# A listed order for the first two groups, own places for chunks 2 to 5, and no unused products at the end

## The chip, the cores and the metric

The kernel runs on one core of a Trainium2 chip. Its time is device microseconds, the median of several runs. The engines are TensorE (PE in the profile, with PEld for its weight loads), VectorE (DVE), ScalarE (ACT), GpSimd (POOL) and SyncE (SP), which here only issues DMAs. Each works off its own queue in order and waits on semaphores for the others.

## The reference

Linear attention with decay, in blocks of 64 positions, feeds a two-layer product with a leaky ReLU. Inputs are q, k, v of (4, 8, 768, 64) in float32, lam per head, and w_in (512, 2048) and w_out (2048, 512) in float64.

```python
for b in range(nb):                       # blocks of 64 positions
    intra = (qb @ kb.T * Dmask) @ vb
    inter = (qb * lam_pow) @ kv_state
    out[b] = intra + inter
    kv_state = lam_block * kv_state + (kb * rev_pow).T @ vb
x = out as (3072 tokens, 512)
h = x @ w_in
g = maximum(0.01 * h, h)
return g @ w_out
```

## The kernel before

**Tiling.** Tokens are cut into 24 chunks of 128 (two blocks each), six to a batch entry; four chunks make a group of 512 tokens, so there are six groups. w_in is cut into eight pairs p of two blocks of 128 columns. The two large products are done in three terms (h, l and m parts of each operand, each rounded to what one pass of PE keeps), so one pair of one group costs 24 matmuls of 128x512: `up(g, p)`, six steps of four matmuls in line L640, two for each of h, l and m. Its result, after the leaky ReLU on ACT (L658, L661), goes through the buffers gs0 and gs1 to DRAM tiles G. After all groups the second product, `down`, reads them back (L700) and writes the output.

**A chunk** goes through these steps. Three loads (k and q as two DMAs of 128 KB each, L338; v as one of 256 KB, L388). `transposes`: k and q are transposed on PE (L403) and copied by ACT (L414, L415); k is scaled in place (L419) and q (L423). `scores`: the scores go to the lower halves of the two banks of psc and the k-v products to the upper halves (both L313); DVE then makes sc (L452) and adds the products to the running state (L457, L459), which POOL scales (L462). `outputs`: own part, first state part, a small read of po (L491), second state part (L313), then xh, xl, xm (L507, L508, L510), which are the moving operand of `up`.

**A half of w_in** (512 KB, one DMA, L566) lands in one of three places raw0 to raw2, is read by ACT three times (L578, L580, L582) and put together by DVE (L584, L585); with two halves there, L591 or L593 makes wh, L596 wl, L602 wm of that pair.

**Places.** k, q, v and their transposed forms of chunk c lie in place c % 2, so a load for chunk c waits until chunk c - 2 has done with them. All loads and stores go through SP's queue, in order.

**Order.** Nothing is issued as it is written. The class `Plan` collects every step with its engine, a cost and the names it reads and writes (`add`); `emit` then picks steps one by one, each time the one that could start first by these costs, and issues them in the order of the planned start times. Names are what it knows of dependencies: psc is one name. Where PE would wait over 0.4 us by the plan, `busy` puts in unused transposes (L266, called fillers here); 11 more run at the very start. Once a pair's product has been put in bank b10, no more are added. The weights come in the order p = 1, 0, 2, 3, 4, 7, 6, 5, and the first `up` is that of group 0 and p = 1, after chunks 0 to 3.

**The end.** After the last step 24 row-strip matmuls (L802) and eight small ones (16 with both halves in the trace, L809) write PSUM areas that nobody reads.

## Time and profile before

| | |
|---|---|
| median of three runs | 611.96 us (610.98 to 612.29) |
| span of the profiled execution | 610.3 us |
| lying around it (median less span) | 1.7 us; no other time of that execution is recorded |
| PE busy, share of the span | 601.9 us, 99% |
| DVE, ACT, POOL busy | 313.2, 269.9, 86.6 us |
| first product in L640 | at 30.41 us |
| unused transposes L266 | 30, the last at 26.8 us |

The page cuts the span into 40 slices; each digit is a busy share in tenths. A busy PE counts unused matmuls too, and matmuls of a stream overlap, so a mean of 389 ns for one of 128x512 stands for one each 227 ns. In the views, "x64" merges neighbours of one kind, and the bracket gives the idle time before an instruction and what ended it.

### The profile page before, as it was taken

To read this page: it belongs to the slowest core of one execution; us is meant where nothing else is said; L and a number is where in the kernel's file an instruction comes from. 1 tells how busy PE (TensorE), PEld (TensorE's weight loads), DVE (VectorE), ACT (ScalarE), POOL (GpSimd) and SP (SyncE) were. 2 spreads that over 40 slices of the span, in tenths; PEclk is the share of its full clock that TensorE was granted. 3 is DMA by queue.
4 is the path that set the end of the run, shared out by engine and by line. 5 is a ranking of instruction groups with operands and counts; after the bars stand their busy time and mean duration, and the time that the engine had idled before them with its cause. 6 is when DMAs were issued, how large, how long until landed. Compare 5 with 4: busy or idle time off the path is not lost.

```text
span 610.3 us, 13012 instructions
## 1 busy us (share of the span) xinstructions
PE 601.9 (99%) x5426; PEld 497.6 (82%) x5426; DVE 313.2 (51%) x418; ACT 269.9 (44%) x430; POOL 86.6 (14%) x90
## 2 busy tenths in 40 slices
PE   7799999999999999999999999999999999999999
PEld 5688888888888878888788888888888888888887
DVE  5899764334243426326366755545454544636531
ACT  4678974444455646555577522222222313214111
POOL 2564412114133004104000000000000000000000
PEclk9899999999999999999999999999999999999999
DMA  9999775666889878886686843524333343333201
GB/s 201 236 261 263 215 204 126 175 154 176 192 212 245 212 222 219 212 242 212 233 302 219 278 155 103 173 69 139 137 104 134 111 136 111 132 104 126 82 1 69
DMA packets 147754, 105.18 MB, mean 172 GB/s; under 512 B 123632, under 2 KB 124400, under 8 KB 147696
## 3 DMA queue, kind: packets, MB, share of 16 engines
q1 hardware_dynamic: 147552, 104.36, 58.8%
q8 instruction: 42, 0.69, 0.5%
q14 instruction: 16, 0.13, 0.1%
q10 hardware_dynamic: 144, 0.00, 0.0%
HBM read 68.69 MB, written 35.65 MB: 171 GB/s over the span
## 4 chain that ended last, share of the span: by engine, by line
PE 95%; DMA 2%; ACT 1%; DVE 1%; issue 0%; SPq 0%; ACTq 0%
PE b L640 42%; PE b L700 18%; PE po L700 11%; PE psc L700 11%; PE po L313 4%; PE psc L313 4%; PE pt L700 4%; DMA g<-gs 1%; DMA att<-in_v_dram 1%; PE pt L403 1%; DMA att<-in_q_dram 1%; PE po L403 0%; PE psc L802 0%; ACT att L415 0%; PE b L266 0%
## 5 line engine op out<-in xcount | busy, mean ns | idle before, releaser
L682 ACT ACTIVATE xh<-att 128x1024 fp32r<-128x1024 f32 x48 | 50.8, 1060 | 149.1 <-PE b L700 133.6
L683 DVE SCALAR_TENSOR_TENSOR xl<-att,xh 128x1024 fp32r<-128x1024 f32 x48 | 58.7, 1223 | 97.5 <-ACT xh L682 97.5
L640 PE MATMUL b<-xm,wm 128*128 128x512 f32 (+2 forms) x392 | 104.5, 392 | 0.7 <-ACT b L658 0.7
L640 PE MATMUL b<-xh,wh 128*128 128x512 f32 (+2 forms) x392 | 103.2, 386 | 0.8 <-ACT xh L507 0.8
L640 PE MATMUL b<-xl,wl 128*128 128x512 f32 (+2 forms) x392 | 103.4, 387 | 0.0
L640 PEld LDWEIGHTS b<-xh,wh 128*128 128x128 f32 x392 | 72.9, 188 | 16.0 <-ACT xh L507 0.9
L640 PEld LDWEIGHTS b<-xl,wl 128*128 128x128 f32 x392 | 72.7, 188 | 15.1 <-DVE wl L596 0.3
L640 PEld LDWEIGHTS b<-xm,wm 128*128 128x128 f32 x392 | 71.4, 188 | 16.0 <-ACT b L658 1.1
L658 ACT ACTIVATE b<-b 128x512 f32<-128x512 f32 (+2 forms) x97 | 56.1, 580 | 60.6 <-PE b L640 60.5
L661 ACT ACTIVATE gs<-b 128x512 f32<-128x512 f32 (+2 forms) x97 | 57.0, 592 | 44.2 <-PE b L640 38.3
L700 PE MATMUL b<-wh,xh 128*128 128x512 f32 x192 | 74.7, 389 | 0.0
L700 PE MATMUL b<-wl,xl 128*128 128x512 f32 x192 | 74.7, 389 | 0.0
L685 DVE SCALAR_TENSOR_TENSOR xm<-xl,xh 128x1024 fp32r<-128x1024 f32 x48 | 58.7, 1225 | 4.7
L462 POOL TENSOR_TENSOR att<-att 128x256 f32<-128x256 f32 x40 | 34.4, 861 | 58.7 <-DVE att L459 58.7
L700 PEld LDWEIGHTS b<-wh,xh 128*128 128x128 f32 x192 | 36.1, 188 | 7.5
L700 PEld LDWEIGHTS b<-wl,xl 128*128 128x128 f32 x192 | 36.0, 188 | 7.5
L423 POOL TENSOR_TENSOR att<-att 128x512 f32<-128x512 f32 (+1 forms) x20 | 25.3, 1265 | 95.6 <-PE po L313 34.7
L452 DVE TENSOR_TENSOR att<-psc,att 128x512 f32<-128x512 f32 x24 | 16.5, 689 | 43.1 <-PE psc L313 43.1
L584 DVE TENSOR_SCALAR w<-w 128x512 int32<-128x512 int32 x32 | 19.6, 612 | 36.0 <-ACT w L578 35.9
L700 PE MATMUL psc<-wh,xh 128*128 128x512 f32 x96 | 37.3, 389 | 0.0
L700 PE MATMUL psc<-wl,xl 128*128 128x512 f32 x96 | 37.3, 389 | 0.0
L700 PE MATMUL psc<-wm,xm 128*128 128x512 f32 x96 | 37.3, 389 | 0.0
(79 smaller groups left out, 810.4 us busy)
## 6 DMA issues: line engine op xcount, KB each, us to landing
att<-g SPq DMA_DIRECT2D x48, 512.0 KB, 3.3
g<-gs SPq DMA_DIRECT2D x47, 512.0 KB, 4.0
raw<-in_moe_w_in_dram SPq DMA_DIRECT2D x16, 512.0 KB, 5.5
raw<-in_moe_w_out_dram SPq DMA_DIRECT2D x16, 512.0 KB, 4.8
att<-in_k_dram SPq DMA_DIRECT2D x48, 128.0 KB, 4.3
att<-in_v_dram SPq DMA_DIRECT2D x24, 256.0 KB, 4.5
out_dram<-gs SPq DMA_DIRECT2D x23, 256.0 KB, 2.1
wo<-w SPq DMA_DIRECT2D x8, 512.0 KB, 5.9
```

The lines of the kernel that those rows point to most:

```text
L313: nc.tensor.matmul(dst[HALF[cols]], lhsT=lhsT[HALF[rows]], rhs=rhs[HALF[rows]], start=start, stop=True, skip_group_check=True)
L423: add(eng, us, lambda: e.tensor_tensor(o, x, _bc(pow_q, 2, 2)[:, :, m, :], op=ALU.mult), ["fq", dep], [f"qsT{i}"])
L452: add("DVE", 0.69, lambda: nc.vector.tensor_tensor(sc, psc[:, :, lower, :], decay, op=ALU.mult), ["psc", "fk"], ["sc"])
L462: add("POOL", 0.7, lambda new=new, j=j: nc.gpsimd.tensor_tensor(state[(j + 1) % 4], new, _bc(lam_c, 2, D), op=ALU.mult), [f"st{j % 4}", "f ...
L584: add("DVE", 0.42, lambda: nc.vector.tensor_scalar(d, d, 3, None, op0=ALU.logical_shift_left), [], [key])
L640: nc.tensor.matmul(dst, lhsT=w[z][:, kk * 2 * P + f * P:kk * 2 * P + (f + 1) * P], rhs=x[z][:, kk, toks], start=start and kk == 0, stop=kk ...
L658: add("ACT", ns, lambda b=b: nc.scalar.activation(out=b, in_=b, func=AF.Copy, bias=0.0, scale=S + 1.0), [], [kb], rank=-1.5)
L661: add("ACT", ns, lambda b=b, r=r: nc.scalar.activation(out=r, in_=b, func=AF.Prelu, bias=0.0, scale=1.0 / WS, alpha=0.01), [kb], [f"gs{jg} ...
L682: add("ACT", 1.05, lambda: nc.scalar.activation(out=h, in_=graw[j], func=AF.Copy, bias=0.0, scale=NEAR), reads, wr("h"))
L683: add("DVE", 1.25, lambda: nc.vector.scalar_tensor_tensor(l, graw[j], 1.0, h.bitcast(F32), op0=ALU.mult, op1=ALU.subtract), reads + [f"rh{ ...
L685: add("DVE", 1.25, lambda: nc.vector.scalar_tensor_tensor(m, l.bitcast(F32), -S, h.bitcast(F32), op0=ALU.mult, op1=ALU.add), [f"rh{j}", f" ...
L700: nc.tensor.matmul(acc[tb][z // 2][:, cols], lhsT=ring[j][z][:, f * T + tb * P:f * T + (tb + 1) * P], rhs=W[pp][z][:, f * d_model:(f + 1) ...
```

## The change

Four things change.

First, `ORDER` lists 711 steps: everything up to the last product of groups 0 and 1, with the loads, weights and attention steps that go with it. A number is a step's place in the order in which `add` was called, a letter says which engine takes it where there is a choice (a ACT, v DVE, p POOL), and f1 or f2 puts one or two fillers ahead of the next PE step. `emit` places these in the listed order, per engine, and goes on by its old rule after them; fillers by rule are off. The list has ten fillers besides the first eleven; the old order had 19.

To read its beginning: 2, 3, 4 are the loads of k, q, v of chunk 0; 25, 26, 27 those of chunk 1; 48, 49, 50 of chunk 2; 71, 72, 73 of chunk 3; 109, 110, 111 of chunk 4; 118, 119, 120 of chunk 5. 94 and 100 load the two halves of w_in's p = 1, 165 and 171 those of p = 0, 203 and 209 those of p = 2, 218 and 224 those of p = 3. 35, 58 and 80 are the k-v products and 34, 57 and 81 the scores of chunks 1, 2 and 3. 159 is the first product. 177 makes wh of p = 0 on DVE and 238 is the first product with it. 9p puts the scaling of chunk 0's k on POOL, where the old run had it on DVE.

The SP order of the loads up to the first product was k0 q0 v0 k1 q1 v1, half of p 1, q2 k2, half of p 1, v2 q3 k3 q4 v3, half of p 0, k4 q5 v4, half of p 0. In the list it is k0 q0 v0 k1 k2 q1 q2, half of p 1, v1 q3 v2, half of p 1, k3 v3, half of p 0, half of p 0, q4, half of p 2, k4.

Second, chunks 2 to 5 get places of their own, in the memory of the weights of p = 5, 6, 7 and 4, which are made last. A step without cost (write names of the chunk and of the weights) hands the memory over.

Third, the scores and the k-v products get names of their own, psS and psK, in place of psc, and the second part of the factors (`factors_q`) names the first as an input.

Fourth, the unused products at the end are gone.

```diff
+ORDER = """
+2 3 4 0 25 f1 5 48 1 9p f1 6 26 8 10 7 f1 12 49 f1 28 94 11 30 32p 27 13 72 14 15 f2 29 51 31 33 50 18 55 16 19
+34 20a 17 21 95 36 52 53 100 22 71 35 54 23 96 73 57 37 56 41 38 42 98 165 43a 39 44 59 58 40 45 97 75 60 46 61
+77 171 99 f1 64 102 110 47 65 101 79 66a 103 f1 67 104 74 68 105 203 76 78 62 106a 109 69 f1 81 63 80 82 83 87
+70 88 107 89a 90 91 108 167 f1 159 166 92 172 154 24 168 113 175 173 209 93 155 118 174 169 160 170 156 111 176
+157 218 161 447 177v 205 112 178 158 238 116 206 162 179 204 210 224 239 84 120 233 134 240 211 234 85 207 119
...
+"""
...
+        for i, e in self.listed:
+            e = e or next(iter(self.ops[i][0]))
+            assert i in able[e]
+            put(i, e, max(free[e], since(i, e)))
...
-                if self.idle is not None and t > soon[e] + 0.4:
+                if i in self.fill:
+                    self.idle(self.fill[i])
+                elif not self.listed and self.idle is not None and t > soon[e] + 0.4:
...
+    OWN = {2: 5, 3: 6, 4: 7, 5: 4}
...
-    W = [[sb([P, 4 * 2 * P], f"w{x}{p}", F32R) for x in "hlm"] for p in range(NP)]
+    def weights(p, dt=F32R):
+        return [sb([P, 4 * 2 * P], f"w{x}{p}", dt) for x in "hlm"]
+
+    W = [weights(p, F32 if p in OWN.values() else F32R) for p in range(NP)]
...
+    for p in OWN.values():
+        for j, (x, y) in enumerate(zip(kqv, (kTs, qTs, qsTs))):
+            z = W[p][j]
+            x.append(z[:, :H * D].rearrange("p (h d) -> p h d", h=H))
+            y.append(z[:, H * D:].rearrange("p (y t) -> p y t", y=HP))
...
-    add("DVE", 1.25, factors_q, [], ["fq"])
+    add("DVE", 1.25, factors_q, ["fk"], ["fq"])
...
-        return c // NCB, c % NCB, c % 2
+        return c // NCB, c % NCB, c % 2 if c not in OWN else 2 + list(OWN).index(c)
...
-            add("PE", 0.47, go, [f"kT{i}", f"qT{i}"], ["psc"])
-        add("PE", 0.47, kv, [f"k{i}", f"v{i}"], ["psc"])
+            add("PE", 0.47, go, [f"kT{i}", f"qT{i}"], ["psS"])
+        add("PE", 0.47, kv, [f"k{i}", f"v{i}"], ["psK"])
...
+        if p in OWN.values():
+            i = 2 + list(OWN.values()).index(p)
+            add("DVE", 0.0, lambda: W[p].__setitem__(slice(3), weights(p)), [],
+                [f"{x}{i}" for x in ("k", "q", "v", "kT", "qT", "qsT")] + [f"w{x}{p}" for x in "hlm"])
...
-    strips(2, 6)
-    strips(4, 3)
-    f = graw[0]
-    for _ in range(4):
-        for i in range(2):
-            nc.tensor.matmul(spare[2][HALF[i], 0:C2], lhsT=f[:, 0:C2], rhs=f[:, 0:C2], start=True, stop=True, skip_group_check=True)
```

More of the change, by code (lines that the diff above doesn't have):

```diff
@@ new lines @@
+157 218 161 447 177v 205 112 178 158 238 116 206 162 179 204 210 224 239 84 120 233 134 240 211 234 85 207 119
+86 212 208 241 115 114 213 127 235 214 128 163 215v 236 220 216 121 237 244 125 135 129 219 249 130 123 217 153
+131 242 245 221 222 225 164 250 117 180 246 132 136 223 251 247 323 226 149 181 252 227 228 122 133 138 229 124
+139 141 126 140a 143 230a 142 152 187 248 231 137 266 144 255 147 145 202 148 260 151 329 150 243 362 232 261
+267 182 262 184 325 195 185 188 186a 189 197 183 190 256 198 193 191 199 324 263 192 194 253 335 420 200 268
@@ new lines @@
+327 257 201 254 146 270 326 301 274 271 273 283 272a 275 328 300 258 276 330 277 350 289 259 278 288 331 290
+333 294 284 291 332 285 295 264 334 269 296 265 292 286 336v 356 287 297 293 337 280 339 196 279 344 338 340
+281 303 341 345 351 352 342 354 346 302 298 304 299 305 308 306v 468 483 309 307 469 310 347 343 311 353 366
+348 375 414 357 349 358 380 360 408 312 484 359 367 355 474 368 470 361 369 435 381 318 370 473 363a 319 376
+382 364 371 377 372 383 365 373 313 374 378 415 482 416 386 379 387 384 410 385 397 409 498 388 391 412 417 418
@@ new lines @@
+392 411 419 413 441 398 393 322 421v 389 480 399 422 477 394 390 475 317 479 402 395 320 314 423 472 403 436
+476 316 437 396 400 478 404 424 471 401 315 442 425 443 445 321 518 439 429 444 282 430 451 460 481 503 431 465
+499 426 458 500 438 456 502 501v 446 504 459 405 509 466 508 510 464 432 440 406 467 461 448v 427 457 449 407
+487 428 452 545 527 550 516 492 463 536 486 454 488 455 450 453 493 489 553 433 549 490 494 537 495 517 491 540
+555 496 462 505 543 560 506 434 561 671 566 589 546 562 515 547 556 485 551 511 497 563 557 526 590 552 538 581
@@ new lines @@
+558 521 591 548 512 592 559 541 513 542 594 593 524 514 564 528 595 567 568 570 588 569v 571 522 577 572 554
+620 573 578 532 596 582 539 579 621 574 529 576 534 625 580 622 533 626 520 544 601 525 604 531 602 519 605
+603v 507 606 530 597 585 523 535 623 598 565 627 599 689 607 631 608 690 619 586 616 628 600 611 691 610 692
+624 583 587 629 584 613 632 633 636 634v 637 650 694 638 648 675 614 693 672 651 695 653 649 659 639 700 661
+617 615 658 612 662 652 705 673 630 646 706 618 666 682 701 707 575 687 696 678 708 702 680 703 679 676 697 665
@@ L37 @@
+677 635 698 660 704 642 654 709 643 688 663 644 609 699 645 640 684 686 647 674 641 664 685 681 710 670 668 657
+655 667 669 656 683
+"""
 class Plan:
@@ L50, in __init__ @@
         self.cold, self.idle, self.spare = 6.0, None, None
+        self.listed, self.fill = [], {}
     def begin(self, name):
@@ L85, in emit @@
         follows, heads = {}, {}
+        first = {i for i, _ in self.listed}
         for c in self.chains.values():
+            if first.issuperset(c):
+                continue
             m = [i for i in c if "PE" in self.ops[i][0]]
@@ L113, in emit, with put @@
         done = []
-        while len(done) < n:
-            best = None
-            for e in free:
-                for i in able[e]:
-                    if e == "PE" and (i != locked[0] if locked else i in follows):
-                        continue
-                    t = max(free[e], since(i, e))
-                    if (best is None or (t, self.ops[i][3]) < best[:2]) and good(i, e, t):
-                        best = (t, self.ops[i][3], i, e)
-            t, _, i, e = best
+        def put(i, e, t):
             ways, fn = self.ops[i][:2]
-            if i in heads:
-                locked = list(heads[i])
-            elif locked and i == locked[0]:
-                locked.pop(0)
             for x in ways:
@@ L143, in emit @@
                         able[x].add(u)
+        for i, e in self.listed:
+            e = e or next(iter(self.ops[i][0]))
+            assert i in able[e]
+            put(i, e, max(free[e], since(i, e)))
+        while len(done) < n:
+            best = None
+            for e in free:
+                for i in able[e]:
+                    if e == "PE" and (i != locked[0] if locked else i in follows):
+                        continue
+                    t = max(free[e], since(i, e))
+                    if (best is None or (t, self.ops[i][3]) < best[:2]) and good(i, e, t):
+                        best = (t, self.ops[i][3], i, e)
+            t, _, i, e = best
+            if i in heads:
+                locked = list(heads[i])
+            elif locked and i == locked[0]:
+                locked.pop(0)
+            put(i, e, t)
         self.timeline = sorted(done)
@@ L152, in emit @@
             if e == "PE":
-                if self.spare in self.ops[i][4]:
+                if self.spare in self.ops[i][4] and not self.listed:
                     self.idle = None
-                if self.idle is not None and t > soon[e] + 0.4:
+                if i in self.fill:
+                    self.idle(self.fill[i])
+                elif not self.listed and self.idle is not None and t > soon[e] + 0.4:
                     self.idle(int((t - soon[e] - 0.2) / 0.22))
@@ L445, in scores @@
         if c < GOFIRST:
-            add("PE", 0.47, go, [f"kT{i}", f"qT{i}"], ["psc"])
-        add("PE", 0.47, kv, [f"k{i}", f"v{i}"], ["psc"])
+            add("PE", 0.47, go, [f"kT{i}", f"qT{i}"], ["psS"])
+        add("PE", 0.47, kv, [f"k{i}", f"v{i}"], ["psK"])
         if c >= GOFIRST:
-            add("PE", 0.47, go, [f"kT{i}", f"qT{i}"], ["psc"])
+            add("PE", 0.47, go, [f"kT{i}", f"qT{i}"], ["psS"])
         def uses():
-            add("DVE", 0.69, lambda: nc.vector.tensor_tensor(sc, psc[:, :, lower, :], decay, op=ALU.mult), ["psc", "fk"], ["sc"])
+            add("DVE", 0.69, lambda: nc.vector.tensor_tensor(sc, psc[:, :, lower, :], decay, op=ALU.mult), ["psS", "fk"], ["sc"])
             for t in range(n_pu):
@@ L456, in uses @@
                 if n == 0 and t == 0:
-                    add("DVE", 0.42, lambda new=new: nc.vector.tensor_copy(new, pu[0]), ["psc"], [f"st{j % 4}"])
+                    add("DVE", 0.42, lambda new=new: nc.vector.tensor_copy(new, pu[0]), ["psK"], [f"st{j % 4}"])
                 else:
                     add("DVE", 0.42, lambda new=new, t=t: nc.vector.tensor_tensor(new, new, pu[t], op=ALU.add),
-                        ["psc"], [f"st{j % 4}"])
+                        ["psK"], [f"st{j % 4}"])
                 if n_pu == 2:
@@ L587, in parts @@
     def parts(p, src, keys):
-        wh, wl, wm = W[p]
+        w = W[p]
         def head(e):
             if e == "ACT":
-                nc.scalar.activation(out=wh, in_=src, func=AF.Copy, bias=0.0, scale=NEAR / S)
+                nc.scalar.activation(out=w[0], in_=src, func=AF.Copy, bias=0.0, scale=NEAR / S)
             else:
-                nc.vector.tensor_scalar(wh, src, NEAR / S, None, op0=ALU.mult)
+                nc.vector.tensor_scalar(w[0], src, NEAR / S, None, op0=ALU.mult)
         add(("ACT", "DVE"), (1.05, 0.7), head, keys, [f"wh{p}"])
-        add("DVE", 1.25, lambda: nc.vector.scalar_tensor_tensor(wl, wh.bitcast(F32), -S, src, op0=ALU.mult, op1=ALU.add),
+        add("DVE", 1.25, lambda: nc.vector.scalar_tensor_tensor(w[1], w[0].bitcast(F32), -S, src, op0=ALU.mult, op1=ALU.add),
             keys + [f"wh{p}"], [f"wl{p}"])
@@ L600, in difference @@
     def difference(p):
-        wh, wl, wm = W[p]
-        add("DVE", 1.25, lambda: nc.vector.scalar_tensor_tensor(wm, wl.bitcast(F32), 1.0, wh.bitcast(F32), op0=ALU.mult, op1=ALU.subtract),
+        w = W[p]
+        add("DVE", 1.25, lambda: nc.vector.scalar_tensor_tensor(w[2], w[1].bitcast(F32), 1.0, w[0].bitcast(F32), op0=ALU.mult, op1=ALU.subtract),
             [f"wh{p}", f"wl{p}"], [f"wm{p}"])
@@ L780 @@
             if not freed:
-                add("DVE", 0.0, lambda: None, [], ATT + [f"gr{j}" for j in range(NR)])
+                add("DVE", 0.0, lambda: None, [], ATT + ["psS", "psK", "psc"] + [f"gr{j}" for j in range(NR)])
                 add("ACT", 0.0, lambda: None, [], [f"raw{j}" for j in range(NRAW)] + ["t0", "t1"])
@@ L789 @@
             down(*x[1:])
-    plan.emit()
-    a, b = ring[0][0], W[0][0]
-    spare = acc[0] + acc[1]
-    def strips(n, times):
-        k = P // n
-        for _ in range(times):
-            for i in range(n):
-                r = slice(i * k, (i + 1) * k)
-                nc.tensor.matmul(spare[i], lhsT=a[r, 0:P], rhs=b[r, 0:T], start=True, stop=True, skip_group_check=True)
-    strips(2, 6)
-    strips(4, 3)
-    f = graw[0]
-    for _ in range(4):
-        for i in range(2):
-            nc.tensor.matmul(spare[2][HALF[i], 0:C2], lhsT=f[:, 0:C2], rhs=f[:, 0:C2], start=True, stop=True, skip_group_check=True)
+    fill = 0
+    for x in ORDER.split():
+        if x[0] == "f":
+            fill = int(x[1:])
+            continue
+        i = int(x.rstrip("avp"))
+        plan.listed.append((i, {"a": "ACT", "v": "DVE", "p": "POOL"}.get(x[-1])))
+        if fill and "PE" in plan.ops[i][0]:
+            plan.fill[i], fill = fill, 0
+    plan.emit()
 _INS = ['q', 'k', 'v', 'lam', 'moe_w_in', 'moe_w_out']
```

## The prediction

> **What bounds the kernel now.** I read the windows view first, cut where the work changes character: before the first k lands, up to the first product of the first matrix (L640), the rest of the first two groups, and the end.

> ```profile
> 0.00:4.04 4.04, 2.61 (x11) 2.21 (x11) 0.57 (x4) 1.28 (x1) 0.74 (x7) 1.00 0.42 93
> 4.04:30.41 26.37, 21.24 (x556) 16.27 (x556) 20.45 (x43) 15.00 (x28) 10.59 (x12) 0.94 1.04 238
> 30.41:128.55 98.14, 98.14 (x1305) 82.88 (x1306) 65.25 (x94) 66.98 (x118) 34.42 (x28) 1.00 0.76 204
> ```

> Columns: length, PE, PEld, DVE, ACT, POOL busy, granted clock, DMA share, GB/s. From 30.41 us on PE is never idle for 98 us; an order of the other engines can win nothing there, only lose. The 26.4 us ahead of it are the stock: PE idle 5.1, another 4.4 in fillers (L266 in the same window), the clock below full once. DMA is full there (share 1.04), so what matters is which bytes come first. The chain of waits says what the end of that stage hung on:

> ```profile
> 19.07 5.23 DMA att<-in_v_dram
> 24.30 0.14 issue
> 24.43 1.57 PE psc L313 x64
> 26.00 1.26 PE b L266 x5
> 27.26 1.39 PE po L313 x48
> ...
> 29.86 0.51 ACT xh L507
> 30.36 0.04 issue
> 30.41 1.66 PE b L640 x6
> ```

> v of chunk 3 comes at 24.3. The queue of SyncE shows why:

> ```profile
> 14.79 3.08 SPq L338 DMA_DIRECT2D att<-in_k_dram  x2
> 17.96 1.01 SPq L338 DMA_DIRECT2D att<-in_q_dram  x2
> 19.07 0.46 SPq L388 DMA_DIRECT2D att<-in_v_dram  x1
> ```

> The two halves of k of chunk 3 occupy it for 3 us (their place is chunk 1's, still in use), and q of chunk 4 goes ahead of that v. Last, when weights are ready against when they are used:

> ```profile
> 35.86 1.43 DVE L593 TENSOR_SCALAR wh<-w 128x1024 fp32r<-128x1024 f32 x1
> 38.24 1.99 PE L640 MATMUL b<-xh,wh 128*128 128x512 f32 x8
> 46.53 1.22 DVE L596 SCALAR_TENSOR_TENSOR wl<-wh,w 128x1024 fp32r<-128x1024 f32 x1
> 47.80 0.50 PE L640 MATMUL b<-xl,wl 128*128 128x512 f32 x1
> ```

> wh of p 0 is done at 37.29 and used at 38.24; wl of p 2 at 47.75 and used at 47.80. So DVE is hardly behind the loads as a bound: starting the products earlier is worth only as much as DVE's weights come earlier too.

> **Loads (own places, new order).** In the old order 11 tensors of 256 KB and two halves of w_in lie up to k of chunk 3, which PE sees at 20.0; up to w_in's second half 8 and 2, used from 15.9. 3.0 + 1.25 per tensor + 1.5 per half gives 19.75 and 16.0. In the list the loads are k0 q0 v0 k1 k2 q1 q2, half, v1 q3 v2, half, k3 v3, and none of them has to wait for a place. So v of chunk 1 comes at 3.0 + 8 x 1.25 + 1.5 = 14.5 (later: two tensors more ahead of it), w_in's second half at 18.5 (2.5 later), k3 at 19.75, v3 at 21.0 (3.3 earlier). That is the near end; the far one is the 0.20 MB per us that the old run reached up to v3 (4.46 MB from 2.2 to 24.4): v3 at 23.1, up to 2.1 later.

> **The head, step by step.** Rows overlap: 26.05 (0.69), 26.65 (0.41), 26.98 (0.68), 27.58 on DVE means 0.60, 0.33, 0.60 each, and 1.13 for the 1024-wide ones; ACT likewise 0.52 for a copy, 0.65 for L580 and L582, 0.59 for L578. v of chunk 1 holds its k-v products to 14.6; w_in's first half (13.25) holds ACT, so DVE starts chunk 1's stretch at 15.0 and then has 5.9 of work in a row: 20.9. ACT after w_in's second half: L580, L578, a look at po, L582, xh of chunk 2, kT of chunk 3, done at 22.5. PE: scores and k-v products of chunk 3 to 23.6. DVE from 21.1: L584, L585, state, xl, sc, state, to 24.3. PE own part and first state part to 25.0; look, second part, xh: first product at 26.25.

> Two things are added. First, the new keys psS and psK let the planner start chunk c+1's scores (lower halves of psc) while DVE still reads chunk c's upper halves. The old run has that case:

> ```profile
> 12.88 1.16 PE L313 MATMUL psc<-att 64*64 64x64 f32 x64 [1.08 <-DVE att L459]
> ```

> These scores waited for a read of the other half. I take it that they still will: state behind the next scores and sc behind the next k-v products, 0.6 in all over the chunks (between 0 and the 1.08 of the row). By the plan's keys alone this would be 0 and the forecast 608.9. [...]

> Second, the clock.

> ```profile
> 11.33:14.74 3.41, 2.33 (x76) 1.89 (x72) 2.95 (x6) 2.92 (x6) 0.62 (x1) 1.00 0.97 197
> 21.57:24.98 3.41, 1.60 (x58) 1.32 (x60) 2.34 (x4) 2.20 (x3) 3.41 (x4) 1.00 1.02 279
> 24.98:28.40 3.42, 3.42 (x92) 2.97 (x87) 2.35 (x4) 1.41 (x2) 1.04 (x2) 0.50 0.80 178
> ```

> A stretch of 3.41 us with PE busy 1.60 was followed by one at half clock, one with 2.33 was not. In the new order PE has some 1.5 of work in 11.33 to 14.74 (it waits for v of chunk 1) and ten fillers instead of 19. At half clock 64 score products took 1.57 for 1.16 and 48 of po 1.46 for 0.93; a whole stretch so costs about 1.3 to 1.4. I take half of it, 0.7, with 0 and 1.4 as ends. [...]

> First product: 26.25 + 0.6 + 0.7 = 27.55 against 30.41.

> **Where the gain is cashed.** From its 24.3 DVE still has 7.4 to wh of p 0 (xm, wl, wm of p 1, xl and two xm, L584, L585 twice each, wh): 31.7; with the 1.3 from above and 0.2 for POOL beside it (L584 takes 0.42 alone, 1.22 beside POOL) 33.2 against PE's first product there at 38.24. PE is there at 27.55 + 5 x 0.907 + two transpose steps of 0.5 = 33.1, so both arrive together. But less has been done by then: the old run had one product step (0.9), two more transpose steps (1.0) and chunk 4's scores (1.0) behind it. 33.2 + 2.9 = 36.1 against 38.24: **2.1 us** earlier. After that wl of p 2 comes 6.5 of DVE work later, at 39.7, and PE wants it 9.7 later, at 42.9: 3.2 of cover where the old run had 0.05. v of chunk 4 is wanted at 38.5; it stands behind p 2's second half, whose place ACT frees at about 30.0, so it is issued three issues of 0.55 later and lands 4.5 after that (section 6 of the page), at 36.2: 2.3 of cover. The moved scaling of chunk 0's k (DVE to POOL, 1.06 for 0.67) lies beside the wait for q and v and costs nothing.

> **The end.** The 32 unused matmuls are last in the chain:

> ```profile
> 608.76 0.62 PE po L809 x16
> ```

> PE ends at 609.39; the last output DMA, issued at 607.26 with 1.7 to landing, at about 609.0. Removing them gives 0.4 (0 to 0.4); the landing is late next, and 0.9 of closing steps stay.

> **Sum.** 2.1 + 0.4 = 2.5: span 610.3 to 607.8. The three runs have a median of 611.96, 1.7 above the span; I keep that: **609.5**.

> **Rivals.** *The head hands nothing on.* DVE waits as long as before (6.7 idle up to 40 us), since v of chunk 1 and w_in come later; its work ahead of wh of p 0 shrinks only by 0.93 (L419 to POOL, one L459 later). wh at 36.4, + 2.9 = 39.3 against 38.24: 1.1 lost, 0.4 won: 612.6. For it: DVE's cover was 0.05. Against: the old 2.1 us DVE wait behind v of chunk 3 is gone.

> *Slower: a load behind a held place.* p 2's second half waits in SyncE's queue for ACT's last read of raw2, with k 5, v 4 and p 3 behind it. From a slip of 2.3 PE stalls one for one. A stall of 2.3 also drops the clock: 3.41 us of 512-wide products at half lose 1.7. 609.5 + 4.0 = 613.5; it breaks even at a stall of 0.8 with the drop. For it: the old wait of 1.79 did exactly that, and a listed order cannot step around a late load.

> *More than forecast.* No half-clock stretch and no wait across the halves: 26.25 stands, and the 1.3 comes back: 608.2; with DVE's 0.2 and a few tenths of waits fewer, 607.6.

> **Numbers.** Forecast 0.48 (own range 607.9 to 611.0), nothing handed on 0.22, slower 0.15, more 0.15. About 0.2% (1.2 us) is what a measurement of this kernel tells from no change: 610.7 and 613.2 are the borders. Faster: 0.15 + nearly 0.45 of the forecast = 0.60; same: 0.22 + the forecast's rest, 0.25; slower 0.15. Range 607.0 to 613.2: the better case with its bound for the loads, and up to where the slower case begins.

> **What would show it.** Right: first L640 at 27 to 28, v of chunk 3 landing near 21 and no longer ahead of PE's longest wait, L593 of p 0 ending near 33, PE without idle from 34 on, the last chain ending in the output DMA 0.4 earlier. Wrong: PE waiting in 30 to 60 for L593, L596 or a load, a clock of 0.5 in a stretch after 28, waits of PE on DMA g at the end of the list, or an unchanged last step.

## The result, and the profile after

| | before | changed |
|---|---|---|
| median | 611.91 us (4 runs, 610.98 to 612.29) | 617.53 us (4 runs, 615.32 to 619.31) |
| ratio | | 1.0098 (1.0072 to 1.0123): 1% slower |
| profiled execution: time, span | not recorded, 610.3 us | 619.31 us, 617.5 us |
| first product (L640, now L698) | 30.41 us | 31.95 us |

The change costs 5.6 us where I forecast a gain of 2.5. The four runs had spans of 613.5, 615.0, 616.4 and 617.5 us at mean granted clocks of 1.000, 0.996, 0.993 and 0.992, and the profiled one is the last. It is 1.8 us above the median of these spans and has the lowest clock.

The windows view of the changed kernel, cut as before, then at the three half-clock stretches of 3.41 us (clock 0.50) and the two stretches that stand ahead of them (columns: length, PE, PEld, DVE, ACT, POOL busy, clock, DMA share, GB/s):

```profile
4.04:30.41 26.37, 19.92 (x521) 15.12 (x520) 15.90 (x39) 11.35 (x21) 7.91 (x10) 0.87 1.00 227
30.41:128.55 98.14, 97.00 (x1211) 79.99 (x1204) 63.58 (x89) 66.74 (x120) 28.90 (x29) 0.98 0.72 190
...
18.31:21.73 3.42, 1.74 (x56) 1.22 (x51) 2.50 (x7) 1.44 (x3) 1.40 (x3) 1.00 0.85 222
21.73:25.14 3.41, 3.26 (x68) 2.48 (x69) 2.54 (x6) 2.58 (x5) 0.14 (x1) 0.50 0.83 227
25.14:28.55 3.41, 2.95 (x69) 2.55 (x69) 1.48 (x3) 2.14 (x3) 1.64 (x2) 0.50 0.81 216
28.55:31.97 3.42, 1.86 (x78) 1.33 (x70) 3.12 (x5) 0.83 (x3) 0.00 (x0) 1.00 0.17 38
31.97:35.38 3.41, 3.41 (x8) 2.72 (x9) 3.34 (x6) 3.41 (x6) 0.00 (x0) 0.50 0.00 0
```

Up to 30.41 us every engine did less than before, DVE 15.9 us in place of 20.5. The first eight products ran at half clock, and DMA moved nothing beside them. The chain of waits of the head:

```profile
15.32 0.33 PE psc L366 x3
15.64 1.05 issue
...
19.14 0.79 issue
...
21.10 0.78 issue
...
26.81 1.98 PE psc L366 x64
```

The load of v of chunk 3 is gone from it, as forecast. Three gaps of PE stand there in its place, in which the view names nothing that PE waited for, and the scores and k-v products of chunk 3 take 1.98 us, most of it at half clock. SyncE's queue after the load of v of chunk 3 (start, length, line):

```profile
16.33 0.51 SPq L441 DMA_DIRECT2D wm<-in_v_dram  x1
...
25.40 1.46 SPq L391 DMA_DIRECT2D wh<-in_k_dram  x2
34.38 0.37 SPq L619 DMA_DIRECT2D raw<-in_moe_w_in_dram  x1
```

It stands still from 26.9 to 34.4 us: p 2's second half waits for raw2, which ACT reads late. That is my rival of the held place. Next, wh of p 0 on DVE's timeline, and the product that uses it on PE's:

```profile
36.77 0.69 DVE L647 TENSOR_SCALAR wh<-w 128x1024 fp32r<-128x1024 f32 x1
```

```profile
31.95 3.68 PE L698 MATMUL b<-xh,wh 128*128 128x512 f32 x8 [0.46 <-ACT xh L560]
...
39.05 1.18 PE L698 MATMUL b<-xh,wh 128*128 128x512 f32 x4
```

wh is done at 37.46 (before 37.29, forecast 33.2) and used at 39.05 (before 38.24). Last, the end of the chain:

```profile
612.95 0.96 PE pt L758 x8
...
613.99 0.42 DVE gs L787
```

From the end of the last product in use to the end of the span it is 617.52 - 613.91 = 3.61 us, before 610.29 - 606.29 = 4.00. The end gained its 0.4; so everything ahead of it lost 7.6 in this execution.

**Where it was lost.** A busy PE hides small waits, so I add up PE's useful work instead. A product of 512 columns counts 0.227 us, one of 128 columns 0.104, a transpose 0.112, an attention product 0.0153, each its usual distance from the next in an undisturbed stretch. The time less that sum is how far PE lags. The table gives the lag against the experiment that kept the old order (own places, no end products), in us, from one profiled execution of each kernel:

| kernel | at 40 us | 100 us | 160 us | 340 us |
|---|---|---|---|---|
| before | 0.5 | -0.2 | -0.2 | 0.8 |
| end alone | -0.6 | -1.2 | -1.2 | -0.9 |
| changed | 4.2 | 4.6 | 7.1 | 8.4 |
| list with 36 fillers | 1.9 | 3.5 | 6.0 | 6.7 |
| the same, halves of p 1 later | 1.1 | 1.8 | 4.6 | 5.2 |
| old head, then the list | 0.9 | 2.0 | 4.6 | 5.2 |
| old order as a list | -0.2 | -0.3 | -0.3 | 3.4 |
| old order, v of chunk 3 first | -0.6 | 0.0 | 0.0 | 0.0 |

The first two rows have the old order on the old memory and differ by 1.0 to 1.7, so a single difference of 1 us in this table says little. There are two places of loss beyond that: the head, and 100 to 160 us, where the four kernels with the later part of the list lose 2.5 to 2.8.

### The profile page after: what moved, and what is told of

It is laid out like the page before. It is cut to its first block, busy times and chain, and to the rows that moved or that the text cites. A ratio compares the mean times of both kernels' runs of the same rounds, so it can differ in the third digit from the quotient of the medians.

```text
span 617.5 us, 12884 instructions
## 1 busy us (share of the span) xinstructions
PE 603.5 (98%) x5377; PEld 496.4 (80%) x5377; DVE 310.1 (50%) x417; ACT 265.2 (43%) x430; POOL 80.5 (13%) x91
## 4 chain that ended last, share of the span: by engine, by line
PE 94%; DMA 2%; SPq 1%; ACT 1%; issue 1%; DVE 0%; DVEq 0%; ACTq 0%
PE b L698 43%; PE b L758 18%; PE po L758 11%; PE psc L758 11%; PE po L366 4%; PE pt L758 4%; PE psc L366 3%; SPq L391 1%; DMA att<-in_v_dram 1%; DMA raw<-in_moe_w_in_dram 1%; PE pt L456 1%; PE po L456 0%; ACT xh L560 0%; ACT w L631 0%; PE b L456 0%
## 5 line engine op out<-in xcount | busy, mean ns | idle before, releaser
L698 PE MATMUL b<-xh,wh 128*128 128x512 f32 (+2 forms) x392 | 105.3, 395 | 0.9 <-ACT xh L560 0.8
L698 PE MATMUL b<-xl,wl 128*128 128x512 f32 (+2 forms) x392 | 102.9, 388 | 0.0
L698 PE MATMUL b<-xm,wm 128*128 128x512 f32 (+2 forms) x392 | 101.7, 392 | 0.1
L698 PEld LDWEIGHTS b<-xh,wh 128*128 128x128 f32 x392 | 72.8, 191 | 17.6 <-ACT xh L560 1.6
L698 PEld LDWEIGHTS b<-xl,wl 128*128 128x128 f32 x392 | 72.6, 188 | 15.1 <-DVE xl L561 0.3
L698 PEld LDWEIGHTS b<-xm,wm 128*128 128x128 f32 x392 | 71.0, 188 | 16.1 <-ACT b L716 1.6
L719 ACT ACTIVATE gs<-b 128x512 f32<-128x512 f32 (+2 forms) x97 | 56.4, 591 | 40.9 <-PE b L698 31.9
L512 DVE TENSOR_TENSOR att<-att,psc 128x256 f32<-128x256 f32 x40 | 16.6, 414 | 59.2 <-PE psc L366 55.9
L758 PEld LDWEIGHTS b<-wh,xh 128*128 128x128 f32 x192 | 36.1, 188 | 7.5
L515 POOL TENSOR_TENSOR att<-att 128x256 f32<-128x256 f32 x40 | 27.4, 686 | 79.8 <-DVE att L512 70.1
L758 PE MATMUL po<-wh,xh 128*128 128x512 f32 x96 | 37.3, 389 | 0.0
L758 PE MATMUL po<-wl,xl 128*128 128x512 f32 x96 | 37.3, 389 | 0.0
```

The source lines that it names most:

```text
L512: add("DVE", 0.42, lambda new=new, t=t: nc.vector.tensor_tensor(new, new, pu[t], op=ALU.add), ["psK"], [f"st{j % 4}"])
L515: add("POOL", 0.7, lambda new=new, j=j: nc.gpsimd.tensor_tensor(state[(j + 1) % 4], new, _bc(lam_c, 2, D), op=ALU.mult), [f"st{j % 4}", "f ...
L698: nc.tensor.matmul(dst, lhsT=w[z][:, kk * 2 * P + f * P:kk * 2 * P + (f + 1) * P], rhs=x[z][:, kk, toks], start=start and kk == 0, stop=kk ...
L719: add("ACT", ns, lambda b=b, r=r: nc.scalar.activation(out=r, in_=b, func=AF.Prelu, bias=0.0, scale=1.0 / WS, alpha=0.01), [kb], [f"gs{jg} ...
L758: nc.tensor.matmul(acc[tb][z // 2][:, cols], lhsT=ring[j][z][:, f * T + tb * P:f * T + (tb + 1) * P], rhs=W[pp][z][:, f * d_model:(f + 1) ...
```

## The experiments

"The kernel before" was run again beside the experiments (medians 611.15 to 611.65 us); the ratios are against that.

**The end alone.**

```diff
-    strips(2, 6)
-    strips(4, 3)
-    ... (and the small products after them)
```

> The kernel before without the unused products at the end, nothing else. My theory (the prediction's): the last step in use ended at 606.29 us and the span at 610.29 before; in the changed kernel's profile these are 613.91 and 617.52, so the end costs 3.61 in place of 4.00. Expected 0.4 us faster than before: 611.5 us. Rival 1, the 3.1 us of PE time that the unused products took all come off: 608.8. Rival 2, the last output's landing sets the end in both: no change.

611.02 us, ratio 0.9989 (0.9976 to 1.0001). The size is that of the prediction; the interval just reaches 1, but the 2.8 of rival 1 are excluded. This kernel at 611.0 is what the others are measured from.

**No list: own places and names, ordered by the planner.**

```diff
-ORDER = """ 2 3 4 0 25 f1 5 ... """
+ORDER = """ """
```

> The changed kernel with an empty list: own places, the names psS and psK and the shortened end stay, and the planner orders all steps by its old rule, with its fillers. Theory A, the listed order is what costs (too little slack on ACT, DVE and SyncE's queue, too few fillers): 610.0 to 612.5, at or below the kernel before, first product at 30 us or sooner, at most one half-clock stretch. Theory B, the own places cost (loads that no longer wait for a place fill the DMA queues, and the gaps of PE in which no wait is recorded, 1.05, 0.79 and 0.78 us in the changed kernel's head, come from that): 614 to 617.5, the same gaps seen again.

620.26 us, 1.0135 (1.0118 to 1.0153): 9.2 above the end alone, above the range of either theory, and worse than with the list. The list makes good 2.7 of what the planner loses.

**Names alone, and places alone, each ordered anew by the planner.**

```diff
-        add("PE", 0.47, kv, [f"k{i}", f"v{i}"], ["psc"])
+        add("PE", 0.47, kv, [f"k{i}", f"v{i}"], ["psK"])
```

> The kernel before without its unused end products (611.0 us in the earlier run) and with the names psS and psK in place of psc; no own places, no list. In the changed kernel and in its version without a list PE still waits between scores and k-v products for DVE's reads of the other half (0.53 us at 12.9, 0.79 at 19.1), although the planner thinks it need not. Theory N: the names make the planner believe in an order that the engines do not keep, and that is most of what the version without a list lost (620.3): here 616 to 620. Theory P, the loss there is the own places': here 610.5 to 611.5.

> The version without a list (620.3 us) with the one name psc back: own places and the shortened end alone, ordered by the planner. Theory N (the names cost): 610.5 to 612. Theory P (the own places cost, with deeper DMA queues and a memory handed over late to the weights of p 4 to 7): 616 to 620.

616.24 us, 1.0083 (1.0064 to 1.0102), and 617.71, 1.0097 (1.0079 to 1.0114). Neither theory holds alone: either edit makes the planner choose another order, and either new order is 5 to 7 us worse. That left open whether the memory itself costs anything.

**Own places under the old order.** The planner is left thinking of two places; all engines and SyncE then work in the old sequence.

```diff
-        return c // NCB, c % NCB, c % 2
+        return c // NCB, c % NCB, c % 2 if c not in OWN else 2 + list(OWN).index(c)
...
-                move(1.15, go, [], [f"{nm}{i}"], issue=1.0)
+                move(1.15, go, [], [f"{nm}{c % 2}"], issue=1.0)
```

> The kernel before without its unused end products (611.0 us), each engine's and SyncE's order exactly as it was, but chunks 2 to 5 in places of their own: the planner still thinks of two places, so only the memory differs, and loads no longer wait for chunk c - 2. Theory O, the order: what costs is that the planner or the list orders the steps anew, and the places as such cost nothing: 610.0 to 611.5. Theory Q, the queue: places of their own let SyncE run ahead, the instruction packets come later behind the loads and PE stops at its 129-record borders: 612.0 to 614.0, with stops of PE that no recorded wait explains.

611.14 us, 0.9998 (0.9989 to 1.0006), 12 runs. Theory O: the places cost nothing. They give nothing either, and SyncE's timeline in this kernel shows that they free no load:

```profile
15.42 2.50 SPq L347 DMA_DIRECT2D wh<-in_k_dram  x2
...
19.06 0.51 SPq L397 DMA_DIRECT2D wm<-in_v_dram  x1
```

The two loads of k of chunk 3 occupy the queue for 2.50 us though their place is free (3.08 in the kernel before, which I had put down to the place; 1.79 in the profile of the end alone, with the old places), and v of chunk 3 lands at 24.25 us against 24.30 and 23.33. So the place was not what held them.

**v of chunk 3 first,** on own places and on the old ones.

```diff
+    plan.moves = [(73, 110, 0), (113, 81, 1), (115, 106, 1), (117, 84, 1)]
```

> Old order and own places (611.1 us), with one thing of the list: v of chunk 3 is loaded ahead of q of chunk 4, and with it the transposes of q of chunk 4 go behind the scores of chunk 3 (PE, ACT, POOL each by one step). There v of chunk 3 landed at 24.25 us and PE began its k-v products at 24.38. This is the first half of my prediction by itself. If it holds, v lands at 21.5 to 22.5, the first product starts 1.0 to 1.5 us sooner than the 29.04 there (27.5 to 28.0), and what it gives at the end is 0.5 to 1.5 us: 609.6 to 610.6. Rival: DVE and ACT, which have the weights of p 1 to make, set the first product, and PE only waits for xh or wh instead: 610.8 to 611.5.

> The same moves on the old memory (kernel before without the unused end products, 611.0 us), no own places. With own places and the old order v of chunk 3 landed at 24.25 us against 24.30 in the kernel before, and the two issues of k of chunk 3 took 2.5 us against 3.1: the place was not what held SyncE's queue. So the same as the run with own places, within 0.4 us. Rival, the prediction's reading that k of chunk 3 waits for its place: v comes 1 us or more later here than with own places, and the gain is lost (611 or more).

611.8 us, 1.0000 (0.9990 to 1.0011), and 611.4, 0.9996 (0.9983 to 1.0009): no gain, the first a little above the rival's range too. v lands at 21.52, 2.7 us sooner than in the same kernel without the move (24.25), and at 21.31, 2.0 sooner than in the end alone (23.33); own places are not needed for it. But the first product starts at 29.10 and 28.84, against 29.04 and 28.54. What came next is in the chain of waits of the first of the two, and then in PE's timeline:

```profile
21.86 1.02 POOL wh L434
22.89 0.04 issue
22.93 1.02 PE psc L328 x51
```

```profile
25.89 0.41 PE L328 MATMUL po<-wm,att 64*64 64x64 f32 x16
26.92 0.85 PE L418 MATMUL pt<-att,wl 128*128 128x128 f32 x4 [0.62 <-DMA wl<-in_q_dram]
27.61 0.38 PE L281 MATMUL b<-att 128*128 128x128 f32 x2
27.92 0.46 PE L328 MATMUL po<-wm,att 64*64 64x64 f32 x16
29.10 2.11 PE L661 MATMUL b<-xh,wh 128*128 128x512 f32 x8 [0.72 <-ACT xh L522]
```

The products of chunk 3 start at 22.93 in place of 24.38, since POOL scales k of chunk 3 until 22.88. Then the transposes of q of chunk 5 stand ahead of the last attention step in PE's queue, and the second half of that q lands at 27.29, in the kernel without the move at 27.30. So 1.3 us of the 2.7 went to POOL's scaling, and the rest to that load, to two fillers behind it, and to ACT's look at po, which stands behind ACT's reads of a half of w_in until 26.90. The rival had nearly the size (its range ends at 611.5), but its reason, xh or wh made late by DVE's weights, is not what held the first product.

In the lag table this kernel is 0.6 ahead at 40 us and level at 100. The end alone is as far ahead at 40 us with nothing moved, and further ahead at 100. So what an earlier first product is worth later is not shown by these profiles; the medians show that this move is worth nothing.

**More fillers: the clock.**

```diff
-77 171 99 f1 64 ... f1 81 63 80 82 83 87
-70 88 107 89a 90 91 108 167 f1 159
+f3 75 ... f3 81 63 80 82 83 f6 87 70 88 107 89a f2 90 91 108 167 f4 159
```

> The changed kernel with 36 fillers in its list in place of 10, put ahead of the PE steps that waited between 12.9 and 31.9 us. Theory C, the clock: four runs of the changed kernel spread over 615.3 to 619.3 us, spans 613.5, 615.0, 616.4 and 617.5 at mean clocks 1.000, 0.996, 0.993 and 0.992; if the fillers keep the clock at full, all runs lie near the first, 615.3 or a little more (616.0 with some fillers in the way), all clocks at 0.997 or above, no half-clock stretch on the first products. Rival D, the half-clock stretches do not follow PE's idle time here: the clocks stay spread as they were, and the median at 617.5 to 619 with the fillers' own time added. What is left above the kernel before (3.4 us with full clock throughout) is in neither case touched.

616.68 us, 1.0075 (1.0059 to 1.0090). All six runs have a clock of 0.999 or 1.000, and their spread is 2.4 us. So theory C is right on this kernel's clock and too low on its time (615.3 to 616.0). The median is 0.85 us lower, less than the two kernels' runs scatter; 5.7 us above the end alone remain at full clock. More fillers are no guarantee: with 46 (below) two of six runs had 0.997 and 0.994. Of the 5.7 us, 1.33 are a stop in PE's timeline, from 64.66 us on:

```profile
65.99 0.27 PE L366 MATMUL psc<-att 64*64 64x64 f32 x1 [1.33 <-issue]
```

**Stops of PE at fixed records.** The trace also lists the 16384-byte packets of a queue that it calls "instruction". Counting the records of PE's weight-load queue, the unexplained stops end at the 229th, the 358th or a later record 129 on, 1.3 to 1.6 us after such a packet has landed:

```
kernel                      record  packet starts, lands   PE goes on
changed                       229      14.01  15.32           16.69
changed                       358      19.32  20.53           21.88
list, 36 fillers              229      13.97  15.29           16.63
list, 36 fillers             1132      63.70  64.72           65.99
list, 46 fillers              229      13.85  15.16           16.66
list, halves of p 1 later     229      13.12  14.44           15.75
no list                       358      16.30  17.25           18.64
held place (below)            358      19.87  21.11           22.57
names alone                   487      21.32  22.59           24.22
```

In none of the 17 traces is one of the first five of these records passed sooner than 1.28 us after its packet has landed; where the packet landed early, as in the kernel before (12.26 for a record at 15.3), there is no stop.

```diff
-7 f1 12 49 ... f2 29 51
+7 f8 12 49 ... f5 29 51
```

> The list with 36 fillers (616.7 us), and 10 more before PE's waits at 7.1 and 10.1 us. In all runs so far PE stops, waiting for nothing that the trace records, at the 229th, 358th (or a later 129th) record of its weight-load queue, 1.3 to 1.4 us after a 16384-byte instruction packet has landed; that packet is asked for, it seems, when the 129 records before are begun, and started 3.4 us later in the changed kernel (behind a half of w_in) against 1.6 before. Theory G, instruction refill: with 10 more records ahead of 9 us the first packet starts at 12.7 or sooner in place of 13.97, the stop of 1.43 us at 15.2 shrinks below 0.5 or goes, and PE reaches the first product up to 1 us sooner. If it stays, it is at the 229th record again, so 10 matmuls earlier in the work. Rival M, the stop belongs to the step (the products that read the new places): it stays at the same matmuls with 1.0 to 1.4 us.

616.83 us, 1.0093 (1.0071 to 1.0116). The stop stayed at the 229th record, ten matmuls earlier in the work, so it does not belong to the step. That is theory G's half. Its other half failed: the packet started at 13.85 us all the same, and the stop was 1.63 us long.

```diff
-28 94 11 30 ... 33 50 18 ... 95 36 52 53 100 22 71 ... 54 23 96 73
+28 11 30 ... 33 50 94 18 ... 36 52 53 22 71 ... 54 23 95 96 73 100
```

> The list with 36 fillers (616.7 us), with the two halves of w_in of p 1 moved back in SyncE's order (behind v of chunk 2, and behind v of chunk 3) and ACT's reads of the first half behind the copies of chunk 2. Moving PE's trigger alone did nothing (616.8): the instruction packet started at 13.85 us whether asked for at 10.6 or 0.7 sooner, just after the first half of w_in, issued at 9.1, had landed at 13.1. Theory G, the packet stands behind the data that were queued before it: now it starts at 11.5 to 12.5, the stop at the 229th record (1.43 us, ending 16.63) goes, and as nothing wants the halves that early the run gains 1.0 to 1.5 us: 615.2 to 615.7. Rival: PE is paced by the chain of waits through DVE and ACT, so the stop only turns into another wait: 616.3 to 617.

616.78 us, 1.0092 (1.0078 to 1.0106): no gain, as the rival has it. PE's timeline in that kernel shows the stop shorter and another wait behind it:

```profile
15.75 0.21 PE L366 MATMUL psc<-att 64*64 64x64 f32 x1 [0.57 <-issue]
...
19.72 0.46 PE L366 MATMUL po<-att 64*64 64x64 f32 x16 [1.84 <-ACT att L544]
```

The packet started only 0.85 us sooner (13.12), and ACT's look at chunk 1 stood behind its read of the half that now came later. In the kernels of the table such a stop took up to 1.96 us (record 358 in the kernel of the held place, below). What starts a packet is open: with ten more records ahead of it, it started at 13.85 us, without them at 13.97.

**The held place.**

```diff
-83 f6 87 70 88 107 89a f2 90 91 108 167 f4 159 166 92 172 154 24 168 113 175 173 209
+107 167 82 83 166 168 209 f6 87 70 88 89a f2 90 91 108 f4 159 92 172 154 24 113 175 173
```

> The list with 36 fillers (616.7 us) and one change of order: DVE makes wl of p 1 ahead of the scores' scaling of chunk 3, where it was idle for 2.2 us, and ACT reads raw2 (first half of p 0) ahead of its look at chunk 3, where it was idle for 2.8. So p 2's second half goes out at about 30 us, not 34.4, and k 5, v 4 and p 3 behind it 4 us sooner. Theory H, the held place in SyncE's queue costs: PE's waits between 50 and 180 us shrink, and the run is 1 to 2 us faster, 614.7 to 615.7. Rival: DMA idle from 29 to 34 us was free time, nothing wants those loads earlier: within 0.5 us of 616.7.

618.30 us, 1.0111 (1.0091 to 1.0131): a miss. In the profile the first product starts at 34.6 us, in place of 31.2, behind a stop of 1.96 us at record 358 and 6.8 us at half clock, and the half went out at 33.0, not at 30; how much of that the edit did is open. The two of its six runs with a clock of 0.999 or more took 616.65 and 617.02, no better than the 616.68 without the move. No sign that the held place costs anything, but no clean test of it.

**Which part of the list.** First the list cut after two product steps; then three lists of the same 711 steps: the old order, the old order's first 168 and then the list's, and the list's first 140 and then the old.

```diff
-... 159 166 92 172 154 24 168 113 ... 669 656 683
+... 159 166 92 172 154
```

> The changed kernel with its list cut after step 154, the second of the first two product steps; the planner orders everything after that by its old rule. I compare the time at which PE has got through a given amount of its own work (products, transposes, attention) in the two profiles: the changed kernel is behind the old one by 3.7 us when the first products are through (40 us) and by 7.6 at the end, most of the second half of that between 50 and 180 us. Theory E, the two halves have causes of their own (the head, and a later order with too little slack): 617.5 - 3 to 4 = 613.5 to 614.5. Rival F, the later half only hands on what the head began (loads and ACT late by 34 us): within 1 us of the changed kernel, 616.5 to 618.5.

```diff
+2 3 4 0 25 26 1 5 27 7 9v 6 94 8 10 f3 11 49 f3 12 28 13 48 30 32p 14 f1 18 19 100 15 29 20a ...
```

> The changed kernel with another list: the same 711 steps in the order in which the kernel before issues them, with its fillers (19). Everything else of the change stays: own places, names, no end products, and the planner goes on after the list by its own rule with those names. Theory O, only the order of the list costs: 610.5 to 612.0, first product at 28.5 to 29.5. Rival, the change costs by something else than that order (the names in the part after the list, the way a list is issued): 613 or more.

> The first 168 of those steps in the old order (those that it plans for the first 38 us), then the list's own order for what is left. Up to 30 us DVE has done 22.0 us of work in the old order and 16.1 in the listed one. Theory H, the list's head is what costs (DVE, ACT and POOL stand idle in it, and all that comes after inherits that): 611 to 612. Rival T, the list's later part costs by itself, with each step issued just when it is wanted: 613 to 615.

> The list's own first 140 steps (up to the first product with p 0), with the 36 fillers, and then the old order for what is left. Theory H: the head's loss stays and grows as DVE's weights come late: 614 to 617. Rival T: only the 2 us that the list's head loses against the old one by 40 us at full clock: 612.5 to 613.5.

The cut list gave 620.05 us, 1.0129 (1.0102 to 1.0156): neither E nor F; the planner goes on worse from there than the list does. The old order as a list gave 615.31, 1.0063 (1.0040 to 1.0086), which is not theory O's number, but the lag table splits it: up to 160 us it is level with the old order (-0.3), and the 3.7 come after the list has ended. So own places, names and the list as such cost nothing up to there. PE's timeline behind it:

```profile
164.41 1.19 PE L698 MATMUL b<-xm,wm 128*128 128x512 f32 x4 [0.67 <-ACT b L716]
166.46 1.20 PE L698 MATMUL b<-xh,wh 128*128 128x512 f32 x4 [0.86 <-ACT gs L719]
```

So something is lost where the planner takes over from a list, in the changed kernel 1.3 from 160 to 340 us. Whether that is the seam, or the planner's order under the new names, which is the rival's "613 or more", no run separates; the names and the places each cost 5 to 7 us where the planner had all steps. The old head with the list's later part gave 615.59, 1.0055 (1.0035 to 1.0075): rival T, just above its range. From 100 to 160 us it loses 2.6, as the lists with their own head do (2.5 to 2.8). ACT's and PE's timelines of the list with 36 fillers show the largest piece of that:

```profile
139.37 1.09 ACT L719 ACTIVATE gs<-b 128x512 f32<-128x512 f32 x2 [2.80 <-DMA g<-gs]
```

```profile
140.02 1.19 PE L698 MATMUL b<-xh,wh 128*128 128x512 f32 x4 [0.60 <-ACT gs L719]
```

ACT waits for the store of gs, and PE for the bank that ACT has not emptied. The rest are pieces under 0.4 us each: between 100 and 160 us PE's matmuls start over 0.04 us later than their usual distance in 35 places of this kernel (4.0 us in all) and in 17 of the old order (1.6), over half of it where PE goes from attention to products or back, six times each way against four. The last of the three, the list's head with the old later part, gave 636.21, 1.0388 (1.0363 to 1.0413), far outside both theories: its lag at 40 us is already 7.9. The two orders do not fit at that seam (PE waits 5.0 us for a load of q that the old order issues later), so it says nothing on the head.

## Why the prediction was wrong

**The loads** were right. v of chunk 1, the second half of p 1, k and v of chunk 3 landed at 14.32, 19.41, 20.17 and 21.58 us (forecast 14.5, 18.5, 19.75, 21.0). "None of them has to wait for a place" was right too, but idle as a reason for gain: the place had not held k of chunk 3 in the old kernel either.

**What bounds the head: the step that failed.** I read from the chain that the end of the head hung on v of chunk 3, and passed the 3.3 us that it was to come sooner on to the first product almost whole (30.41 to 27.55). The chain gives the last wait, not what the wait is worth. With v alone 2.7 us sooner the first product did not move; POOL's scaling and the load of q of chunk 5 were next. The list takes that q out of the way; there the chain of waits of the head runs mostly through PE's own steps and stops, and DVE stands behind PE. The windows by tens of us, first of the old order (the end-only kernel), then of the changed one:

```profile
10.00:20.00 10.00, 7.96 (x259) 6.38 (x251) 7.50 (x13) 6.82 (x15) 4.46 (x6) 1.00 1.04 244
20.00:30.00 10.00, 8.40 (x218) 6.34 (x217) 9.52 (x14) 6.85 (x13) 7.16 (x7) 1.00 1.05 254
```

```profile
10.00:20.00 10.00, 6.91 (x224) 5.50 (x227) 5.11 (x11) 4.49 (x10) 3.54 (x5) 1.00 1.13 255
20.00:30.00 10.00, 7.94 (x199) 6.31 (x203) 6.18 (x12) 5.20 (x9) 2.26 (x3) 0.66 0.75 210
```

In this execution of the old order DVE works 9.52 of 10 us from 20 on (8.32 on own places, 7.86 in the kernel before). In the list it works 6.18, since it stands behind PE's steps:

```profile
17.49 0.42 DVE L512 TENSOR_TENSOR att<-att,psc 128x256 f32<-128x256 f32 x1 [1.98 <-PE psc L366]
...
28.82 0.69 DVE L505 TENSOR_TENSOR att<-psc,att 128x512 f32<-128x512 f32 x1 [2.20 <-PE psc L366]
```

My walk had DVE "5.9 of work in a row" from 15.0.

**The walk's terms.** Waits across the halves of psc: forecast 0.6, measured 0.53 at 12.9 and 0.79 at 19.14 (PE's queue waits there for DVE's semaphore, which rises when DVE has read the scores at 19.83), so 1.3:

```profile
12.89 0.69 PE L366 MATMUL psc<-att 64*64 64x64 f32 x32 [0.53 <-DVE att L512]
```

Clock: forecast 0.7, half the price of a stretch behind 11.33 to 14.74. That one stayed whole (PE busy 2.82 in it). The three that came stand behind 18.31 to 21.73 and 28.55 to 31.97, with 1.74 and 1.86 of PE; the last is my sign of "a clock of 0.5 in a stretch after 28". By the table they cost some 2.3 in this execution by 40 us (4.2 against 1.9 with 36 fillers). More unused transposes went with a higher clock, though not cleanly: it was 0.999 or above in one of four runs of the changed kernel, with 26 more of them in six of six, with 36 more in four of six, and with 26 more and the halves of p 1 moved in two of four. Not in the walk at all: the stops at records 229 and 358, 1.05 + 0.78. Of the 4.4 us between 27.55 and 31.95 these stops are 1.8 and the longer waits across the halves 0.7; the rest, clock included, I did not take apart.

**Where the gain is cashed.** wh of p 0 came at 37.46, not 33.2. My rival "the head hands nothing on" had it late too (36.4), but took DVE to wait as long as before; DVE worked 25.8 us up to 40 us, in the end alone 31.2.

**The later part.** I wrote that an order "can win nothing there, only lose" between 30 and 128 us, and then gave that loss no price. It is 2.5 us between 100 and 160 us, and 1.3 behind that. This is the second failed step, a term put at nothing without a reason: the list was judged on its first 40 us.

**The end** was right (0.39 in the profile, 0.6 by the medians with 1 still in the interval). **The rival of the held place** happened as described (SyncE stands to 34.4 us) and PE showed no wait of over 0.5 us for it; the kernel got slower by other means.

So 6.4 us lie between the changed kernel (617.53) and the old order on the same memory (611.14). By the medians 0.85 of them is clock, within the scatter of the runs. The other 5.5 are order, the list's and the planner's behind it: by the row with 36 fillers some 2 in the head, 2.5 between 100 and 160, the rest between and after.

## What to carry to other kernels

Before pricing a wait that is to go, ask which engine or load is next, and try it alone: one load moved ahead tells in one run what the chain of waits cannot. When a whole order is replaced, price all of it, the seam with what follows too, and not only the stage that it was made for. Keep an order fixed to see what a change of memory or names does by itself: under a planner any edit of a name is also another order, here worth 5 to 9 us. And read a chain of waits from the instruction that you ask about: one that ends in DVE's last step says nothing on PE's first product.
